# DeltaNet with a low-rank mixer on one core: the first two units multiply by Z inside the recurrence

## The chip, the core and the metric

The kernel runs on one core of a Trainium2 chip. The metric is the device time of one execution in microseconds. A measured time is the median of several runs. The profile is of one further execution. All numbers are FP32.

## The reference

For each of 4 batches and 8 heads, a delta rule runs over 768 tokens with a 48 x 48 state. Its output, with the heads side by side (384 columns), goes through a low-rank mixer over the tokens and a two-layer MLP over the channels.

```python
k_n = k / (norm(k) + 1e-6)
for t in range(S):
    y[t] = q[t] @ state
    v_old = k_n[t] @ state
    state = state + beta[t] * outer(k_n[t], v[t] - v_old)
x = heads_side_by_side(y)              # (4, 768, 384)
h = x.transpose(0, 2, 1) @ U @ V       # U: 768 x 32, V: 32 x 768
u = x + h.transpose(0, 2, 1)
out = u + maximum(u @ w_ch1, 0) @ w_ch2   # 384 -> 1536 -> 384
```

## The kernel before

**Chunks and units.** The 768 tokens of a batch are 12 chunks of 64. Six chunks are a unit, so units 0 and 1 are batch 0, units 2 and 3 are batch 1, and so on to unit 7. A unit's data live in one of two slots, which alternate. In each chunk the kernel forms k k^T (`pg`) and the masked k q^T (`qk`), inverts the triangular matrix that the delta rule gives (the result is called Z, 64 x 64 for each head and chunk; it overwrites `pg` and is then read as `zt`), and then runs over the chunks one after the other with the state.

**The inverse.** `blocks` solves 32 x 32 diagonal blocks, for units 0 to 2 as pairs of 16 x 16 blocks, by a chain of VectorE instructions (L803, L809) between two transposes (L794, L816). `joins` puts blocks together with small products. For units 0 and 1 two 16 x 16 blocks are joined by 64-row products in two diagonal quadrants of TensorE's array (L860 first, L874 second, 16 moving columns each). Two 32 x 32 blocks are then joined by L900, L903, L918 and L921. `part` and `diagonals` make copies on ScalarE for this. `place_of`, `begin` and `need` only say which step may follow which.

**Ahead of the recurrence.** `prepare`, called for each half of a unit (three chunks), multiplies by Z once: k^T Z (L1023, copied over `kq` by ScalarE) and Z v (L1034, copied over `vn` by ScalarE).

**The recurrence.** `recur` takes the 12 chunks of a batch in turn. For each chunk there is a product of the prepared keys with the old state (L1072), a subtraction from the prepared v on VectorE (L1085), which gives z, a product of k with z (L1100), and an addition to the state on VectorE (L1111). Beside it `outputs` makes the chunk's output: q with the old state (L983) and `qk` with z (L997), which accumulate in one bank, and two copies on ScalarE to X (L967).

**Heads and row halves.** Eight heads are named by j (2), par (2) and g (2). A product of 64 x 64 or 48 x 64 fills one quadrant of the 128 x 128 array: its input rows choose the row half, its output rows the column half. Before the change a head with par = 1 changes its row half on the way (`half(g ^ par)`), so that L1034 and L997 use all four quadrants. L1100 then needs k of those heads on the other half too, which is a second copy, `kz`, loaded by the loads named z.

**The MLP.** When batch 0's outputs are all in X, `front` applies the mixer (L1393, L1399, L1412) and transposes X for a group of 256 tokens (L1436, L1439). `channels` is the first layer (L1497), `narrow` the second, in fewer block products by sums of blocks (L1617). Batch 3 takes its own path (L1296). The weights come as 64-bit numbers and are converted to FP32 by ScalarE (L1198) and VectorE (L1212, L1219, L1226) in `load_weights`, in the first part of the execution.

**What sets the order.** Every piece of work is a generator, and a list written out in the file, `ORDER`, says at which of some 2250 places each generator takes its next step. The steps are issued in this order, so each engine's instructions, and each DMA queue's, stand in it. The times that the steps carry (`op("pe", 0.23, ...)`) were for a planner that made the list; in the build they decide nothing but the list's bookkeeping.

In the profile an FP32 product is two TensorE instructions and a transposition one, so a step of `recur` shows 16 matmuls, a block of L700 (`products`) 48, and one half's `prepare` 48 and 48.

## Time and profile before

| | |
|---|---|
| timed runs, median | 599.51 us (597.67 to 601.25, three runs) |
| the profiled execution | 596.6 us |
| its span in the profile | 594.9 us |
| mean granted TensorE clock | 0.943 |
| TensorE matmul busy | 559.7 us (94%), 10428 instructions |
| VectorE busy | 409.3 us (69%), 1011 instructions |
| ScalarE busy | 216.8 us (36%), 442 instructions |
| GpSimd busy | 133.3 us (22%), 229 instructions |
| DMA moved | 36.23 MB |

The page of the profile has 40 slices of the span, each with the busy tenths of every engine and the granted TensorE clock; groups of instructions by source line; and the chain of work that ended last, followed back from the end. Queries of the trace give the same for a window of time, and a timeline. PE is TensorE's matmuls and PEld its weight loads, DVE is VectorE, ACT ScalarE, POOL GpSimd, SP the queue that issues most DMAs. Matmuls are pipelined: a matmul's own duration is longer than the distance from its start to the next one's start.

### The profile page before, as it was taken

The page shows a single profiled execution, that of the slowest core. Times are in us where ns is not written, and L with a number is a line of the kernel's source. Part 1 is how long each engine was busy: PE and PEld are TensorE (multiplying, and loading weights), DVE is VectorE, ACT ScalarE, POOL GpSimd, SP SyncE. Part 2 cuts the span into 40 slices and gives each one's busy share as a digit, 9 for nine tenths or more (in the row PEclk, how much of TensorE's full clock was granted, in tenths as well). Part 3 has the DMA queues.
Part 4 walks back from the last instruction along what each step waited for, and adds up shares of the span by engine and source line. Part 5 has one row for each costly group of instructions (what it writes and reads, how often), then busy time and mean ns, then how long its engine had stood idle before and what let it go on. Part 6 is the DMA issues. An engine that isn't in the chain of part 4 may idle for free.

```text
span 594.9 us, 23426 instructions
## 1 busy us (share of the span) xinstructions
PE 559.7 (94%) x10428; PEld 481.6 (81%) x10428; DVE 409.3 (69%) x1011; ACT 216.8 (36%) x442; POOL 133.3 (22%) x229
## 2 busy tenths in 40 slices
PE   3778978899999999999999999999999999999997
PEld 3578977678988887989889887889899868656997
DVE  3888758899999458999884279998883235313542
ACT  1846475446322542035224341252243321335000
POOL 8122036116010724141205214520310000000000
PEclk9855556999999999999999999999999999999999
DMA  9981639714030415240402144420401000000000
GB/s 140 180 176 24 214 80 197 152 56 79 3 65 12 68 31 92 46 91 13 82 2 43 18 83 90 79 56 2 95 7 43 4 2 4 16 8 1 26 28 28
DMA packets 89445, 36.23 MB, mean 61 GB/s; under 512 B 75456, under 2 KB 87104, under 8 KB 89344
## 3 DMA queue, kind: packets, MB, share of 16 engines
q1 hardware_dynamic: 80800, 24.69, 20.7%
q0 software_dynamic: 6944, 9.74, 8.3%
q8 instruction: 82, 1.34, 1.0%
q10 hardware_dynamic: 1600, 0.30, 0.3%
q14 instruction: 19, 0.16, 0.1%
HBM read 29.98 MB, written 4.72 MB: 58 GB/s over the span
## 4 chain that ended last, share of the span: by engine, by line
PE 83%; DVE 11%; issue 2%; ACT 2%; DMA 1%; SPq 0%; DVEq 0%; ACTq 0%
PE P L1617 27%; PE P L1497 22%; PE P L1296 7%; PE P L700 4%; DVE xt L809 3%; DVE prod L803 3%; PE P L1072 2%; PE P L860 2%; PE P L874 2%; PE P L1023 2%; PE P L1034 2%; PE P L983 2%; PE P L997 2%; PE P L1100 2%; PE P L1412 2%
## 5 line engine op out<-in xcount | busy, mean ns | idle before, releaser
L1497 PE MATMUL P<-ut,w_sb 128*128 128x256 f32 x648 | 150.1, 385 | 1.5 <-ACT ut L1439 0.9
L1497 PEld LDWEIGHTS P<-ut,w_sb 128*128 128x128 f32 x648 | 119.9, 190 | 18.7 <-ACT ut L1439 1.1
L1617 PE MATMUL P<-w_sb,hs 128*128 128x192 f32 x540 | 96.7, 331 | 0.1
L1617 PEld LDWEIGHTS P<-w_sb,hs 128*128 128x128 f32 x540 | 87.2, 190 | 3.7 <-issue 1.2
L809 DVE TENSOR_TENSOR xt<-xt,prod 128x112 f32<-128x112 f32 (+21 forms) x200 | 64.6, 323 | 6.9
L803 DVE TENSOR_TENSOR prod<-gs,xt 128x112 f32<-128x112 f32 (+21 forms) x200 | 63.3, 316 | 3.5
L1537 DVE TENSOR_TENSOR X<-X,P 128x192 f32<-128x192 f32 x84 | 29.1, 349 | 49.8 <-PE P L1617 49.4
L1462 ACT ACTIVATE hs<-P 128x512 f32<-128x512 f32 x54 | 32.2, 598 | 77.5 <-PE P L1497 65.6
L967 ACT COPY X<-P 64x192 f32<-64x192 f32 x96 | 30.0, 313 | 66.3 <-PE P L997 63.4
L1617 PE MATMUL P<-w_sb,S 128*128 128x192 f32 x288 | 50.7, 330 | 0.0
L1617 PEld LDWEIGHTS P<-w_sb,S 128*128 128x128 f32 x288 | 46.6, 190 | 2.8 <-issue 1.8
L555 POOL DMA_DIRECT2D slot<-in_v_dram x32 | 21.1, 664 | 92.3 <-DVE prod L803 60.3
L1085 DVE TENSOR_TENSOR z<-slot,P 128x192 f32<-128x192 f32 x44 | 15.5, 352 | 30.8 <-PE P L1072 29.7
L541 POOL DMA_DIRECT2D slot<-in_q_dram x40 | 24.6, 621 | 46.9 <-DVE slot L747 33.3
L939 ACT COPY slot<-zz 32x384 f32<-32x384 f32 x64 | 32.4, 509 | 7.0 <-DVE zz L878 3.9
L700 PE MATMUL P<-slot 48*64 48x64 f32 x1536 | 30.9, 231 | 2.1 <-issue 1.4
L1296 PE MATMUL P<-slot,w_sb 128*128 128x384 f32 x96 | 32.9, 486 | 0.0
L700 PEld LDWEIGHTS P<-slot 48*64 48x64 f32 x1536 | 27.9, 144 | 5.6 <-issue 2.7
L946 POOL MEMSET slot<- 32x384 f32 x32 | 13.3, 421 | 84.2 <-PE P L903 63.4
L1617 PE MATMUL P<-w_sb,slot 128*128 128x192 f32 x180 | 30.4, 327 | 0.9 <-DVE X L1537 0.9
L555 POOL DMA_DIRECT2D slot<-in_k_dram x44 | 29.4, 670 | 8.3 <-PE P L1100 7.6
L1617 PEld LDWEIGHTS P<-w_sb,slot 128*128 128x128 f32 x180 | 29.3, 190 | 1.7 <-DVE X L1537 1.5
(153 smaller groups left out, 901.4 us busy)
## 6 DMA issues: line engine op xcount, KB each, us to landing
out_dram<-X SPq DMA_DIRECT2D x22, 192.0 KB, 2.7
w_sb<-in_moe_w_ch_dram SPq DMA_DIRECT2D x10, 384.0 KB, 5.6
slot<-in_k_dram SPq DMA_DIRECT2D x48, 72.0 KB, 3.9
slot<-in_k_dram POOLq DMA_DIRECT2D x44, 72.0 KB, 3.8
slot<-in_v_dram SPq DMA_DIRECT2D x32, 72.0 KB, 3.7
slot<-in_v_dram POOLq DMA_DIRECT2D x32, 72.0 KB, 3.5
X<-in_moe_w_ch_dram SPq DMA_DIRECT2D x6, 384.0 KB, 6.1
wide<-in_moe_w_ch_dram SPq DMA_DIRECT2D x6, 384.0 KB, 5.0
```

What stands on the lines that cost most here:

```text
L541: queue.dma_start(out=blocked(n)[quarter(y % 4), j, g, :, 0:w], in_=src[b, 4 * g + 2 * j + par, hf * UC * L : (hf + 1) * UC * L, BK * low ...
L555: queue.dma_start(out=t[half(1 - g if name == "z" else g), :, to, 0:D], in_=src[b, 4 * g + s, hf * UC * L : (hf + 1) * UC * L, :].rearrang ...
L700: nc.tensor.matmul(p_g[half(g ^ (par * i)), par, c], kq[rows, c, j, 0, half(g)], kq[rows, c, j, i, half(g)], start=True, stop=True,)
L803: nc.vector.tensor_tensor(out=prod, in0=gb[:, :, j : j + 1, j + 1 :].to_broadcast([128, split, m, w]), in1=xb[:, :, 0:m, j : j + 1].to_bro ...
L809: nc.vector.tensor_tensor(out=xb[:, :, 0:m, j + 1 :], in0=xb[:, :, 0:m, j + 1 :], in1=prod, op=ALU.subtract,)
L939: nc.scalar.copy(pg[quarter(i), :, at, :, a : a + BK], cut(zc, h)[quarter(i)].rearrange("p r (c j) t -> p r c j t", j=2),)
L967: nc.scalar.copy(x[half(c % 2), c // 2, 4 * D * g : 4 * D * (g + 1)].rearrange("p (j r d) -> p r j d", r=2, d=D), states(p_y)[half(g)],)
L1296: nc.tensor.matmul(to, w, t, start=start, stop=stop, skip_group_check=True)
L1462: nc.scalar.activation(hs[:, fs[0] : fs[1] + 1 : fs[1] - fs[0]], p_f, ACTF.Relu)
L1497: nc.tensor.matmul(p_f[:, x], w(x, t), ut[:, t], start=(t == 0), stop=(t == KT - 1))
L1537: nc.vector.tensor_tensor(out=to, in0=to, in1=p, op=ALU.add)
L1617: nc.tensor.matmul(to, of[0], of[1], start=of[2], stop=of[3], skip_group_check=True)
```

## The change

For units 0 and 1 (`DIRECT`) `prepare` does nothing. Instead `recur` multiplies by Z in each chunk, after the subtraction: z = Z (v - k S), one product of eight heads more, and a copy on ScalarE. For the same units (`NATURAL`) heads keep their row half from beginning to end; `kz` is not loaded, and the products of Z and of `qk` use two diagonal quadrants. The first join products of units 0 and 1 run on 32 moving columns instead of 16, of which the second 16 are read. The diagonal of `xt` is written by ScalarE in a step of its own, `spread`, for all units. The two masking instructions of a `qk` block become one. Two fillers are added: a product of the identity with itself, 256 columns, whose result is not read. The list `ORDER` is written anew for all steps (2253 instead of 2259): it begins with unit 0's k, and the recurrence of batch 0 begins straight after the joins of unit 0. The diff, without the list:

```diff
--- before.py
+++ after.py
@@ -141,210 +141,210 @@
+    FILLERS = (0, 1)
     ORDER = """
...
@@ -502,6 +502,8 @@
     TURNED = 3
     TURNED_K = 3
     SPLIT, QUARTERED = (0, 1), (2,)
+    DIRECT = (0,1)
+    NATURAL, ONCE = (0, 1), ()
     FIRST = dict(k1=11, q0=12, q1=13, z0=14, v0=15, z1=16, v1=17)
     FIRST = {(x[0], int(x[1])): y for x, y in FIRST.items()}
 
@@ -608,6 +610,13 @@
     def landed(name, n, j=1):
         return need(*[(name, n, g, j) for g in range(2)])
 
+    def spread(n):
+        yield op("act", 0.2)
+        nc.scalar.copy(
+            out=xt.rearrange("p s t -> p (s t)")[:, 0 : BK * BK : BK + 1], in_=cp[:, n % 2]
+        )
+        emitted(("spread", n), 0.06)
+
     def norms(n):
 
         _, _, _, _, _, vn, _, _ = units[n]
@@ -618,15 +627,13 @@
         norm = small.tile([128, BK], FP32, name="norm")
         nc.scalar.sqrt(norm, flat[:, 0 : BK * BK : BK + 1])
         yield need(("betas", hf))
-        yield op("dve", 1.25, port=True)
+        yield op("dve", 1.05, port=True)
         nc.vector.tensor_scalar_add(norm, norm, 1e-6)
         rec = small.tile([128, BK], FP32, name="rec", bufs=1)
         nc.vector.reciprocal(rec, norm)
         nc.vector.tensor_tensor(out=rec, in0=rec, in1=rec, op=ALU.mult)
         nc.vector.tensor_tensor(out=cp[:, n % 2], in0=rec, in1=betas[:, hf, b], op=ALU.mult)
-        nc.vector.tensor_copy(
-            out=xt.rearrange("p s t -> p (s t)")[:, 0 : BK * BK : BK + 1], in_=cp[:, n % 2]
-        )
+        begin(spread(n), 2)
         emitted(("c", n))
         yield op("dve", 0.2)
         rows = small.tile([128, BK], FP32, name="norm_rows")
@@ -698,7 +705,7 @@
                 for par, g in QUADS:
                     rows = half(par, D)
                     nc.tensor.matmul(
-                        p_g[half(g ^ (par * i)), par, c],
+                        p_g[half(g ^ (par * i * (n not in NATURAL))), par, c],
                         kq[rows, c, j, 0, half(g)],
                         kq[rows, c, j, i, half(g)],
                         start=True,
@@ -726,14 +733,13 @@
                         pg[:, :, :, j, at], even[:, y : y + 1],
                     )
             else:
-                for par in range(2):
-                    yield op("dve", dve(384), give=[("pair", x)] if par else ())
-                    nc.vector.tensor_tensor(
-                        out=qk[:, par, :, j],
-                        in0=p_g[:, par],
-                        in1=mask_u[:, None, :].to_broadcast([128, UC, L]),
-                        op=ALU.mult,
-                    )
+                yield op("dve", dve(768), give=[("pair", x)])
+                nc.vector.tensor_tensor(
+                    out=qk[:, :, :, j],
+                    in0=p_g,
+                    in1=mask_u[:, None, None, :].to_broadcast([128, 2, UC, L]),
+                    op=ALU.mult,
+                )
             emitted(("product", n, j, i), 0.1)
 
         def turn_blocks(j, i):
@@ -796,6 +802,7 @@
         yield need(("c", n), ("returned", n - 1))
         yield op("dve", dve(1024 // split), port=True)
         nc.vector.tensor_tensor(out=gb, in0=gb, in1=by, op=ALU.mult)
+        yield need(("spread", n))
         for j in range(size - 1):
             m, w = j + 1, size - 1 - j
             yield op("dve", 2 * dve(split * m * w) + 0.04, port=True)
@@ -848,25 +855,26 @@
                 else:
                     emitted(("parted", n, h))
                 words, mode = (48, "Q") if lone else (96, "J")
+                at = 0 if lone else SB
                 pb = lone and alone(n).rearrange("p c j t -> p (c j) t")
                 for y, e in enumerate(es):
                     if y % 6 == 0:
-                        got = yield op("pe", 0.69 if lone else 0.41, mode, take=None if y else "pair", words=words, flow=0.08 if lone else 0.16, cold=1.7 if lone else None)
+                        got = yield op("pe", 0.69 if lone else 0.41, mode, take=None if y else "pair", words=words, flow=0.16, cold=1.86 if lone else None)
                     if y == 0:
-                        x, p_e = got, one(got)[:, 0 : 12 * SB].rearrange("p (e t) -> p e t", e=12)
+                        x, p_e = got, one(got)[:, 0 : 12 * BK].rearrange("p (e t) -> p e t", e=12)
                     for rows in map(half, range(2)) if lone else map(quarter, range(4)):
                         a = rows.start % L
                         of = pb[rows, e] if lone else heads(pg)[rows, e, a : a + BK]
                         nc.tensor.matmul(
-                            p_e[rows, y], of, zc[rows, e, SB:BK], start=True, stop=True
+                            p_e[rows, y, at:BK], of, zc[rows, e, at:BK], start=True, stop=True
                         )
                 yield op("act", act(192), give=[("pair", x)], rush=True)
                 xe = xz[:, h].rearrange("p c (h t) -> p (c h) t", h=2)
-                nc.scalar.copy(xe, p_e)
+                nc.scalar.copy(xe, p_e[:, :, SB:BK])
                 yield need(("parted", n, h))
                 for y, e in enumerate(es):
                     if y % 6 == 0:
-                        got = yield op("pe", 0.69 if lone else 0.41, mode, take=None if y else "pair", words=words, flow=0.08 if lone else 0.16, cold=1.7 if lone else None)
+                        got = yield op("pe", 0.69 if lone else 0.41, mode, take=None if y else "pair", words=words, flow=0.08 if lone else 0.16, cold=1.86 if lone else None)
                     if y == 0:
                         x, p_d = got, one(got)[:, 0 : 12 * SB].rearrange("p (e t) -> p e t", e=12)
                     for rows in map(half, range(2)) if lone else map(quarter, range(4)):
@@ -990,10 +998,10 @@
                     )
                 emitted(("y1", b, c))
                 yield need(("z", b, c), ("b", b, c if cu == UC - 1 else c + 1))
-                yield op("pe", 0.23, "Q", words=32, flow=0.16)
+                yield op("pe", 0.35 if n in NATURAL else 0.23, "Q", words=32, flow=0.16)
             z = zs[c]
             for j, par, g in heads:
-                at = half(g ^ par)
+                at = half(g ^ par * (n not in NATURAL))
                 nc.tensor.matmul(
                     states(p_y)[half(g), par, j],
                     qk[at, par, cu, j],
@@ -1015,6 +1023,9 @@
 
             kn, kq, zt, _, _, vn, _, _ = units[n]
             yield need(("upper", n, h), ("diagonal", n, h), ("grams", n), ("scaled", n), *landed("k", n, 0), *landed("k", n))
+            if n in DIRECT:
+                emitted(("ready", n, h))
+                return
             cs = range(3 * h, 3 * h + 3)
             x = yield op("pe", 0.70, "Q", take="pair", words=96, flow=0.64)
             p_k = pair(x)[:, :, 0:384].rearrange("p g (c j t) -> p g c j t", c=3, j=2)
@@ -1032,7 +1043,7 @@
             for c in range(3):
                 for j, par, g in heads:
                     nc.tensor.matmul(
-                        p_v[half(g ^ par), par, c, j * D : j * D + D],
+                        p_v[half(g ^ par * (n not in NATURAL)), par, c, j * D : j * D + D],
                         zt[half(g), par, cs[c], j],
                         vn[half(g), cs[c], 2 * par + j],
                         start=True,
@@ -1057,20 +1068,21 @@
         yield need(("rec", NU * b - 1))
         for c in range(NC):
             n, cu = NU * b + c // UC, c % UC
-            kn, kq, _, _, _, vn, _, kz = units[n]
-            yield need(("ready", n, cu // 3), *landed("z", n))
+            kn, kq, zt, _, _, vn, _, kz = units[n]
+            direct = n in DIRECT
+            yield need(("ready", n, cu // 3), *landed("k" if n in NATURAL else "z", n))
             if cu == UC - 1:
                 begin(outputs(c, s_old), 2 if b == 0 else 60)
                 yield need(("y1", b, c))
             if c == 0:
                 zs[c] = vn[:, cu]
                 emitted(("b", b, c))
-            else:
+            if c > 0:
                 xb = yield op("pe", 0.23, "Q", take="pair", words=32, flow=0.16)
                 p_b = pair(xb)[:, :, 0 : 2 * D]
                 for j, par, g in heads:
                     nc.tensor.matmul(
-                        states(p_b)[half(g ^ par), par, j],
+                        states(p_b)[half(g ^ (0 if direct or n in NATURAL else par)), par, j],
                         kq[half(par, D), cu, j, 0, half(g)],
                         states(s_old)[half(par, D), g, j],
                         start=True,
@@ -1079,15 +1091,32 @@
                 emitted(("b", b, c))
                 if cu < UC - 1:
                     begin(outputs(c, s_old), 2 if b == 0 else 60)
-                yield need(("y", b, c - 3)) if c > 2 else []
+                yield need(("y", b, c - 3)) if c > 2 and not direct else []
                 yield op("dve", dve(192), give=[("pair", xb)])
-                z = zs[c] = small.tile([128, 4, D], FP32, name="z", bufs=3)
+                z = vn[:, cu]
+                if not direct:
+                    z = zs[c] = small.tile([128, 4, D], FP32, name="z", bufs=3)
                 nc.vector.tensor_tensor(
                     out=z.rearrange("p (r j) d -> p r (j d)", r=2),
                     in0=vn[:, cu].rearrange("p (r j) d -> p r (j d)", r=2),
                     in1=p_b,
                     op=ALU.subtract,
                 )
+            if direct:
+                xz = yield op("pe", 0.35 if n in NATURAL else 0.23, "Q", take="pair", words=32, flow=0.16)
+                p_z = pair(xz)[:, :, 0 : 2 * D]
+                for j, par, g in heads:
+                    nc.tensor.matmul(
+                        states(p_z)[half(g ^ par * (n not in NATURAL)), par, j],
+                        zt[half(g), par, cu, j],
+                        vn[half(g), cu, 2 * par + j],
+                        start=True,
+                        stop=True,
+                    )
+                yield need(("y", b, c - 3)) if c > 2 else []
+                yield op("act", act(192), give=[("pair", xz)], rush=True)
+                z = zs[c] = small.tile([128, 4, D], FP32, name="z", bufs=3)
+                nc.scalar.copy(z.rearrange("p (r j) d -> p r (j d)", r=2), p_z)
             emitted(("z", b, c))
             if c == 0:
                 begin(outputs(c, None), 2 if b == 0 else 60)
@@ -1096,10 +1125,10 @@
                 xs = yield op("pe", 0.23, "Q", take="pair", words=32, flow=0.16)
                 p_s = pair(xs)[:, :, 0 : 2 * D]
                 for j, par, g in heads:
-                    at = half(g ^ par)
+                    at = half(g ^ par * (n not in NATURAL))
                     nc.tensor.matmul(
                         states(p_s)[half(par, D), g, j],
-                        kz[at, cu, j] if par else kn[at, cu, 2 * j, 0:D],
+                        kz[at, cu, j] if par and n not in NATURAL else kn[at, cu, 2 * j + par, 0:D],
                         zs[c][at, 2 * par + j],
                         start=True,
                         stop=True,
@@ -1439,6 +1468,13 @@
         nc.scalar.copy(to, p_u)
         emitted(("front", b, i), 0.1)
 
+    def filler(k):
+        x = yield op("pe", 0.44, "F", take="pair", words=4, flow=0.427)
+        nc.tensor.matmul(
+            one(x)[:, 0:256], ident, ident[:, None, :].to_broadcast([128, 2, 128]), start=True, stop=True
+        )
+        free["pair"][x] = state["now"] + 0.06
+
     def reserve():
 
         yield [("x", 0, NC - 2)]
@@ -1648,11 +1684,13 @@
             begin(grams(n, 1), place_of(n) + 3)
             begin(blocks(n), place_of(n))
             for y, name in enumerate("bkqvz" if n >= TURNED_K else "kqvz"):
-                if n or y:
+                if (n or y) and not (name == "z" and n in NATURAL):
                     for some in ((0,), (1,)) if n < NU else ((0, 1),):
                         begin(load(n, name, some), FIRST.get((name, n), 20 + 4 * n + y))
         begin(load_weights(), 40)
         begin(reserve(), 0)
+        for k in FILLERS:
+            begin(filler(k), 0)
         begin(weight_sums(), 97)
         begin(token_sums(), 3)
         begin(first_of_last(), 94)
```

405 lines of the change are left out of this document (202 added, 203 removed).

## The prediction

> **What bounds the kernel now.** I read the page's 40 slices first, then the busy time by stretch, the groups of single lines, the timeline of a few microseconds, and the chain that ended last. The slices show an ending that is full and a beginning that is not:
>
> ```profile
> PE   3778978899999999999999999999999999999997
> PEclk9855556999999999999999999999999999999999
> ```
>
> A slice is 14.9 us. From slice 8 on TensorE is busy at full clock; in slices 3 to 6 it is nearly as busy, but the granted clock is half. The same by stretch (length, then busy time and instructions of PE, weight load, DVE, ACT, POOL, then the clock):
>
> ```profile
> core 0: us, PE busy (x) PEld busy (x) DVE busy (x) ACT busy (x) POOL busy (x), PEclk, DMA share, GB/s
> 0.00:34.20 34.20, 17.12 (x386) 14.94 (x386) 21.48 (x73) 15.94 (x30) 15.69 (x33) 0.92 1.13 169
> 34.20:50.50 16.30, 14.82 (x433) 14.45 (x433) 13.35 (x38) 10.20 (x22) 6.00 (x11) 0.50 0.51 100
> 50.50:58.30 7.80, 7.09 (x246) 6.81 (x243) 7.22 (x21) 4.11 (x6) 1.74 (x3) 0.50 0.18 42
> 58.30:86.40 28.10, 25.52 (x804) 24.40 (x808) 19.44 (x36) 16.33 (x36) 2.60 (x6) 0.50 0.46 144
> 86.40:107.80 21.40, 16.93 (x613) 14.69 (x605) 16.45 (x31) 13.24 (x25) 12.13 (x20) 0.76 0.87 197
> 116.00:500.00 384.00, 380.40 (x7393) 330.16 (x7394) 290.40 (x723) 133.63 (x274) 92.53 (x155) 1.00 0.23 46
> ```
>
> From 116 us PE idles 3.6 us in 384. The built order of both kernels has the same 494 PE steps from `channels b0 i0 e0` on, with the same 138 changes between full-array and quadrant work, so I give that part no gain and no loss. What the change can move is the start of the first L1497 product, now at 115.95 us, and everything behind it shifts by as much.
>
> Before it lie: start-up to 34.2 (loads, then DVE's substitution of unit 0), the joins of unit 0, `prepare` of unit 0, the joins of unit 1 mixed with the recurrence of batch 0, the rest of the recurrence, the front. The chain shows what carries these:
>
> ```profile
> 3.89 4.96 DMA slot<-in_k_dram
> 18.66 1.98 DVE gs L794
> 34.19 5.30 PE P L860 x96
> 55.76 1.28 PE P L1023 x45
> 57.04 1.25 PE P L1034 x45
> ```
>
> L860, a 64x64 product in one of two diagonal quadrants with 16 moving columns, takes 5.30 us for 96, so 55 ns each. L1023 and L1034, the same size in all four quadrants, take 1.28/45 = 28 ns. Both are at half clock. So a quadrant accepts one instruction each 107 to 110 ns whatever moves through it, and two quadrants give half the rate of four. Full clock shows the same ratio: L588 in two quadrants takes 0.70 us of starts for 24 (29 ns), L1072 in four 14 ns. This is my price for all products that the change puts on two quadrants.
>
> One recurrence step at half clock:
>
> ```profile
> 97.26 0.68 PE L983 MATMUL P<-s,slot 48*64 48x48 f32 x16
> 97.35 0.35 DVE L1085 TENSOR_TENSOR z<-slot,P 128x192 f32<-128x192 f32 x1 [0.40 <-PE P L1072]
> 97.75 0.58 PE L1100 MATMUL P<-z,slot 64*48 64x48 f32 x16
> 98.49 0.35 DVE L1111 TENSOR_TENSOR s<-s,P 128x192 f32<-128x192 f32 x1
> 98.98 0.68 PE L1072 MATMUL P<-s,slot 48*64 48x48 f32 x16 [0.22 <-DVE s L1111]
> ```
>
> L1072 starts at 96.53 and again at 98.98: 2.45 us for state product, DVE, update product, DVE. L983 and L997 fill PE's waits.
>
> **The change part by part** (against the profiled execution: span 594.9, 596.6 us in all).
>
> *Start-up.* The new order issues unit 0's k first: its second SP load is the second in that queue, not the fifth (issue at 1.6 instead of 3.89 us; the landing then took 4.96 us). PE's first transposes can start near 6 us, not 9.05, but unit 1's k and the second pair of heads still have to land (fifth to seventh on SP, 3.9 to 5.3 us plus about 5). L794 needs only unit 0's two products; I put it at 16 to 17 us, not 18.66. Two L713 (0.4 us each) and L603 (0.3) of other steps then stand in front of the norms on DVE, while weight conversions (1.0 us in all) leave the substitution. Joins of unit 0 start 2.2 us earlier (bounds 0 and 4): **-2.2**. The two fillers are full-array products on 256 columns: like L1497 (223 ns a start at full clock), two instructions each, 0.9 us at half clock. The first lies in the wait for unit 1's k; the second in a stretch in which PE idled 2.73 us before L860. Zero; uncovered, 0.9 us each.
>
> *First join products on 32 columns.* L700 moves 64 columns at the same 28 ns in four quadrants as L983 moves 48, and L860 moves 16 at the two-quadrant rate, so the quadrant's 107 ns hides 32: zero.
>
> *Unit 0 to unit 1's joins.* Before, 24.1 us from 34.2 to 58.26. `prepare` of unit 0 goes: 192 instructions at 27 ns, 5.1 us. In its place chunk 0 gets its Z product and its output in two quadrants (0.85 each) and its update (0.43) ahead of unit 1's joins: net -3.0. Three L700 blocks now lie in this stage instead of two (1.3): -1.7. And unit 1's joins wait for L816 of unit 1 (2.0 us), which waits for unit 0's last join copies. I take **-1.5** (bounds -3.0 and 0).
>
> *Joins of unit 1 and chunks 1 to 5.* PE was busy 25.5 of 28.1 us here. Added: five Z products, 16 instructions at 53 ns, 4.3 us; five outputs from 0.43 to 0.85, 2.1 us; gone: one L1023 block, 1.3 us. Net 5.1, of which I let idle time swallow 1.5: **+3.6** (bounds 2.0 and 5.1).
>
> *Chunks 6 to 11.* Here the chain decides. Z comes behind the DVE subtraction: 0.85 of starts and 0.25 of drain (0.68 less 0.43 in L983), then an ACT copy like L865 (0.32) and two handovers of 0.05: 1.52 us a chunk, so 2.45 becomes 3.97. Six times: 9.1. The copy also queues on ACT behind weight conversions (L1198, 0.92), as L967 does. Gone is unit 1's `prepare`, which stretched three chunks from 2.45 to 3.7, 2.9 and 3.1: 2.4 us. Once the transposes of unit 2 have run the clock is 1.0, as at 103.5 before: -1.0. Net **+5.7** (bounds 2 and 8).
>
> *The rest.* The front's tt copy (L1399) now stands behind three substitution steps of unit 2 on DVE, where before there was none: 1.3 us, of which I let 1.0 lie beside the front's first products L1393 (2.1): **+0.3**. The eight z loads, ACT's prepare copies (0.8 and 0.64), the diagonal copy moved from DVE to ACT (0.2 each, which DVE awaits only after the 0.65 of L798) and the two mask products made one are off the chain: zero. If ACT is late, each of eight copies costs at most 0.2.
>
> Sum: -2.2 - 1.5 + 3.6 + 5.7 + 0.3 = +5.9, so 602.5 for an execution like the profiled one. That one lies 2.9 below the median of the timed runs (599.51; 597.67 to 601.25). Part of this is luck that I already withhold from the new kernel: the clock stood at 1.0 from 86.4 to 93.2 amid the recurrence. I add 1.0 for the rest: **603.5 us**.
>
> **The clock.** It changes on a grid of 3.41 us. The stretch from 83.0 held L1023 x48 and 72 other small products and was followed by 1.0; the stretches from 52.3 and 55.7, with 20 and 15% less streamed through the array, were followed by 0.5. The profile's stretch from 60 to 70 us has PE busy 10.00 us of 10 at 0.50. The Trainium skill, "TensorE: Matmul & The Clock Gate", part 1, says that one window of about 3.4 us of sustained busy work gives the full clock. The trace disagrees, if busy is read as the busy row: ten busy microseconds of small products got none. I go by the amount streamed.
>
> **The rivals.**
>
> A, *the clock rises and stays* (faster). In the new order two blocks of L700 and all 32x32 joins of unit 0 stand close together just before chunk 0; they stream about as much per 3.41 us as the stretch at 83.0. If the clock rises there and 32-column joins keep it, the 31 us of joins and chunks 1 to 5 shrink to about 21, bound by the chain: -10, so 593.5. It decides if three or more grid stretches between 45 and 80 us show 1.0. Against it: a chunk with five products streams 5/4 of before's, but in 3.97 instead of 2.45 us, and before's was too little. Chance 0.15. By the skill's rule above this would be the likely case.
>
> B, *two quadrants run as fast as four* (near no change). Then Z and outputs cost 0.43 instead of 0.85: 2.1 + 2.1 us less in chunks 1 to 5, 6 x 0.43 = 2.6 less on the chain, 0.8 at chunk 0: 596. L860 and L588 against L983 speak against it. The Trainium skill, same page, part 3 ("What overlaps and what doesn't"), says that a weight load overlaps running products only when its row group differs. By that rule four quadrants, with two row groups, gain nothing over two diagonal ones, which is this rival; the 55 against 27 ns disagree. Chance 0.10.
>
> C, *the earlier start pays for it*: start-up at -4, `prepare` at -3.0, joins at +2.0, chain at +5: 0.3 over the profiled execution with the front's term, with the 1.0 some 598 to 601. Chance 0.17.
>
> D, *ACT becomes the bound of the chain*: a conversion of 0.92 and two output copies of 0.31 before each Z copy would make a chunk 5 us: +6 more, 609. ACT was busy 13.2 of 21.4 us there, so some of this is likely, all of it not. Chance 0.08.
>
> My forecast keeps 0.50.
>
> **How the numbers follow.** A measurement of this kernel can tell about 0.5% (3 us) from no change. Faster than 596.5: nearly all of A and a third of B, 0.18. Within 596.5 to 602.5: C, the rest of B, and the lowest fifth of the forecast, 0.35. Slower: 0.47. The range 595 to 609 leaves out most of A and the tail of D.
>
> **What would show it.** L1497's first start near 121 us (119 to 125). New Z products of 16 in 0.85 us of starts at half clock; if 0.43, B. Update to update near 4 us in chunks 6 to 9, not 2.45. The clock at 0.50 from about 35 to 105 us; if 1.0 for ten of them, A. First join products 55 ns with 32 columns. PE from the first L1497 to the end unchanged within 2 us: if that part moves by more, the place of my whole sum is wrong.

## The result, and the profile after

The changed kernel takes 603.14 us (median of 22 runs, 599.47 to 605.02), the kernel before 599.89 us (22 runs, 595.18 to 602.75): a ratio of 1.0059, 95% interval 1.0038 to 1.0079. It is slower by about 3 us, where 603.5 was forecast. The profiled execution after took 603.8 us with a span of 601.8; before, 596.6 and 594.9.

The slices of the page after, TensorE and its granted clock:

```profile
PE   5888898999999999999999999999999999999997
...
PEclk9655555899999999999999999999999999999999
```

A slice is now 15.0 us. The stretch at half clock is one digit longer than before and TensorE is busier in it. The same by stretch, cut where start-up, unit 0's joins, unit 1's joins with chunks 1 to 5, chunks 6 to 11 and the front end (columns as before the change):

```profile
core 0: us, PE busy (x) PEld busy (x) DVE busy (x) ACT busy (x) POOL busy (x), PEclk, DMA share, GB/s
0.00:32.60 32.60, 20.57 (x342) 17.59 (x343) 20.99 (x70) 13.34 (x26) 16.36 (x34) 0.82 0.82 129
32.60:55.20 22.60, 20.56 (x578) 19.80 (x580) 20.12 (x55) 14.49 (x31) 4.36 (x8) 0.50 0.39 106
55.20:86.00 30.80, 28.71 (x758) 27.26 (x752) 20.04 (x36) 16.13 (x37) 1.65 (x4) 0.50 0.51 159
86.00:113.90 27.90, 23.69 (x605) 21.32 (x606) 19.87 (x33) 14.92 (x34) 6.49 (x10) 0.62 0.50 108
113.90:123.20 9.30, 7.96 (x147) 5.52 (x147) 7.03 (x23) 3.57 (x8) 6.56 (x11) 0.85 0.65 115
123.20:500.00 376.80, 373.77 (x7348) 325.15 (x7349) 286.37 (x701) 132.81 (x276) 94.81 (x159) 1.00 0.25 48
```

The first product of the first layer (L1497 before, L1533 now) starts at 123.19 us, 7.24 later than at 115.95. Behind it nothing has changed: 478.9 us before, 478.6 after.

| us, from the two traces | before | after | difference | forecast |
|---|---|---|---|---|
| start to unit 0's first join | 34.20 | 32.55 | -1.65 | -2.2 |
| to unit 1's first join | 24.06 | 22.61 | -1.45 | -1.5 |
| to the update of chunk 5 | 27.3 | 31.0 | +3.6 | +3.6 |
| to the last output product | 22.0 | 27.5 | +5.5 | +5.7 |
| to the first L1533 | 8.35 | 9.59 | +1.2 | +0.3 |

The sum is +7.2 between these two executions, of which the one before lies 3.3 us below its median and the one after 0.7 above its own. The medians differ by 3.25.

A chunk of the second half, from the timeline after (start, duration, engine, line; in brackets the idle time and what ended it):

```profile
92.47 0.74 DVE L1241 TENSOR_SCALAR w_sb<-power 128x768 int32<-128x768 int32 x1
...
92.61 1.09 PE L1109 MATMUL P<-slot 64*64 64x48 f32 x16
...
93.25 0.96 DVE L1248 SCALAR_TENSOR_TENSOR w_sb<-w_sb 128x768 int32<-128x768 int32 x1
93.77 0.32 ACT L1119 COPY z<-P 128x192 f32<-128x192 f32 x1 [2.62 <-PE P L1109]
...
94.14 0.57 PE L1129 MATMUL P<-z,slot 64*48 64x48 f32 x16 [0.45 <-ACT z L1119]
...
94.50 0.95 PE L1005 MATMUL P<-z,slot 64*64 64x48 f32 x14
94.78 0.35 DVE L1140 TENSOR_TENSOR s<-s,P 128x192 f32<-128x192 f32 x1 [0.58 <-PE P L1129]
```

The Z product (L1109) and ScalarE's copy stand in the chain as forecast, 1.53 us from 92.61 to 94.14. Updates follow each other in 3.9 to 4.1 us up to chunk 9; the last takes 7.6, because unit 2's transposes and products stand before it, as they did before the change (7.0). Note the two conversions of weights on DVE (L1241, L1248): they run while Z is formed.

### The profile page after: what moved, and what is told of

It is laid out like the page before. It is cut to its first block, busy times and chain, and to the rows that moved or that the text cites. A ratio compares the mean times of both kernels' runs of the same rounds, so it can differ in the third digit from the quotient of the medians.

```text
span 601.8 us, 23034 instructions
## 1 busy us (share of the span) xinstructions
PE 572.9 (95%) x10240; PEld 494.1 (82%) x10240; DVE 409.8 (68%) x987; ACT 216.2 (36%) x454; POOL 130.2 (22%) x225
## 4 chain that ended last, share of the span: by engine, by line
PE 87%; DVE 8%; issue 2%; ACT 1%; DMA 1%; SPq 0%; DVEq 0%; ACTq 0%
PE P L1653 28%; PE P L1533 22%; PE P L1325 7%; PE P L707 4%; PE P L1005 3%; PE P L1084 3%; PE P L1129 2%; DVE xt L816 2%; PE P L991 2%; DVE prod L810 2%; PE P L868 2%; PE P L882 2%; PE P L1109 2%; PE P L1034 1%; PE P L1465 1%
## 5 line engine op out<-in xcount | busy, mean ns | idle before, releaser
L1533 PE MATMUL P<-ut,w_sb 128*128 128x256 f32 x648 | 150.5, 385 | 1.0 <-ACT ut L1468 0.9
L1533 PEld LDWEIGHTS P<-ut,w_sb 128*128 128x128 f32 x648 | 119.8, 190 | 18.5 <-ACT ut L1468 1.1
L816 DVE TENSOR_TENSOR xt<-xt,prod 128x112 f32<-128x112 f32 (+21 forms) x200 | 64.6, 323 | 6.9
L1498 ACT ACTIVATE hs<-P 128x512 f32<-128x512 f32 x54 | 32.1, 598 | 71.2 <-PE P L1533 59.2
L1140 DVE TENSOR_TENSOR s<-s,P 128x192 f32<-128x192 f32 x40 | 14.0, 351 | 29.0 <-PE P L1129 27.2
L1099 DVE TENSOR_TENSOR z<-slot,P 128x192 f32<-128x192 f32 x33 | 11.5, 349 | 31.9 <-PE P L1084 31.7
```

Source lines behind the costliest of these rows:

```text
L816: nc.vector.tensor_tensor(out=xb[:, :, 0:m, j + 1 :], in0=xb[:, :, 0:m, j + 1 :], in1=prod, op=ALU.subtract,)
L1498: nc.scalar.activation(hs[:, fs[0] : fs[1] + 1 : fs[1] - fs[0]], p_f, ACTF.Relu)
L1533: nc.tensor.matmul(p_f[:, x], w(x, t), ut[:, t], start=(t == 0), stop=(t == KT - 1))
```

## The experiments

The stages are those of the table above, read from one trace of each kernel: the first join of unit 0 and of unit 1, the update of chunk 5, the last output product, the first product of the first layer, and what is left from there to the end.

| | joins 0 | joins 1 | chunk 5 | last output | first layer | left |
|---|---|---|---|---|---|---|
| before | 34.20 | 58.26 | 85.6 | 107.60 | 115.95 | 478.9 |
| after | 32.55 | 55.16 | 86.1 | 113.60 | 123.19 | 478.6 |
| four_quadrants | 32.41 | 54.67 | 84.3 | 109.09 | 117.76 | 478.9 |
| no_z | 30.44 | 52.58 | 79.6 | 105.24 | 114.56 | 481.6 |
| before_row_half | 32.60 | 56.46 | 84.2 | 106.22 | 114.34 | 479.7 |
| before_z_inside | 32.79 | 56.66 | 88.6 | 115.99 | 124.10 | 485.3 |
| no_fillers | 33.77 | 56.25 | 87.3 | 114.89 | 123.12 | 480.1 |
| fq_prepare | 32.75 | 56.68 | 85.9 | 113.24 | 122.78 | 481.3 |
| after_prepare | 32.70 | 57.88 | 87.5 | 115.11 | 124.44 | 481.6 |
| fq_direct0 | 31.67 | 53.83 | 83.7 | 109.54 | 127.04 | 485.8 |
| direct0 | 32.51 | 55.21 | 84.8 | 114.37 | 131.65 | 485.8 |

**four_quadrants: the changed kernel with heads changing their row half again.**

```diff
-    NATURAL, ONCE = (0, 1), ()
+    NATURAL, ONCE = (), ()
...
+    for at, name in ((211, "load n1 namez halves(0,)"), (153, "load n1 namez halves(1,)"), (119, "load n0 namez halves(1,)"), (112, "load n0 namez halves(0,)")):
+        ORDER[at:at] = [name] * 2
```

> The changed kernel with one part undone: heads with par = 1 change their row half again, so Z products and outputs of units 0 and 1 use four quadrants, and the second copy of k is loaded again (eight loads). Two quadrants are the price (the forecast's row, 55 against 27 ns): each Z product and each output falls from 0.85 to 0.43 us of starts at half clock; 2.1 + 2.1 us in chunks 1 to 5, 6 x 0.43 = 2.6 on the chain, 0.8 at chunk 0, so 5 to 8 us less than the changed kernel, 595 to 598. If two quadrants run as fast as four (rival B), or if the new order is what costs, it stays within 2 us of the changed kernel, 601 to 605.

599.35 us, ratio to before 1.0008 (0.9981 to 1.0036): 3.8 us less than the changed kernel, where 5 to 8 were expected. The whole loss of the change is gone, though Z is still inside the recurrence. Groups of matmuls between 55 and 108 us of this kernel, the Z product and the output (in the fence after it, the same two of the changed kernel between 55 and 112 us):

```profile
L1113 PE MATMUL P<-slot 64*64 64x48 f32 x164 | 7.3, 299 | 1.2 <-DVE slot L1103 0.5
...
L1009 PE MATMUL P<-z,slot 64*64 64x48 f32 x144 | 6.0, 304 | 1.3 <-issue 1.3
```

```profile
L1109 PE MATMUL P<-slot 64*64 64x48 f32 x164 | 10.8, 294 | 1.0 <-DVE slot L1099 0.5
L1005 PE MATMUL P<-z,slot 64*64 64x48 f32 x146 | 9.9, 303 | 1.3 <-issue 1.3
```

One product lasts as long (299 and 294 ns, 304 and 303), yet the busy time of the group falls from 10.8 to 7.3 and from 9.9 to 6.0 us, since more of them run at once. Of these 7.4 us the path gave back 4.5 by the last output (113.60 to 109.09), and the medians 3.8. Chunks 6 to 11 gave back the 2.6 us that were priced (27.5 to 24.8); unit 1's joins with chunks 1 to 5 gave back only 1.4 of 4.2 (31.0 to 29.6), though TensorE's busy time there fell by 3.1 us (28.71 to 25.64). A pause of 1.2 us named "issue", which the changed kernel's trace doesn't have there, takes most of what is missing from those 3.1.

**no_z: the changed kernel with the Z product and its copy in the recurrence left out** (so the state is not the reference's).

```diff
-                    nc.tensor.matmul(
-                        states(p_z)[half(g ^ par * (n not in NATURAL)), par, j],
-                        zt[half(g), par, cu, j],
...
-                z = zs[c] = small.tile([128, 4, D], FP32, name="z", bufs=3)
-                nc.scalar.copy(z.rearrange("p (r j) d -> p r (j d)", r=2), p_z)
+                z = zs[c] = vn[:, cu]
```

> The changed kernel without the multiplication by Z in the recurrence of units 0 and 1: neither the product nor ScalarE's copy is issued, z is v - kS itself. This leaves a part of the computation out. If the chain is what the change lengthened, a chunk goes from about 4.0 to 2.45 us: 9.1 us over chunks 6 to 11, 4.3 of PE time in chunks 1 to 5, 1 at chunk 0; 12 to 15 us less than the changed kernel, 588 to 591. If the earlier start and the order decide and the chain is covered (rival C), 3 to 8 us less, 595 to 600.

599.15 us, ratio 1.0003 (0.9977 to 1.0029). Far from the 588 to 591 that the price list gave, and inside the 595 to 600 that were named for a covered chain (rival C). Up to chunk 5 the price held: from unit 1's first join, 27.0 us instead of 31.0, and five Z products were priced at 4.3. From there to the last output it did not: 25.7 us instead of 27.5, where 9.1 were priced. The timeline of this kernel, one chunk:

```profile
85.94 1.01 DVE L1232 TENSOR_SCALAR w_sb<-power 128x768 int32<-128x768 int32 x1
...
86.07 0.57 PE L1120 MATMUL P<-slot 64*48 64x48 f32 x16
...
86.98 0.96 DVE L1239 SCALAR_TENSOR_TENSOR w_sb<-w_sb 128x768 int32<-128x768 int32 x1
87.86 0.35 DVE L1131 TENSOR_TENSOR s<-s,P 128x192 f32<-128x192 f32 x1
...
88.26 0.68 PE L1084 MATMUL P<-s,slot 48*64 48x48 f32 x16 [0.77 <-DVE s L1131]
```

The update product L1120 is done at 86.64; the addition to the state, which needs only that, starts at 87.86, because the two conversions of weights stand before it in DVE's order. In the changed kernel the same two lines (L1241, L1248) lay under the Z product and its copy. So Z's 1.5 us on the chain was in good part time in which DVE did work that must be done in this stretch anyway. What was gained was partly lost once more behind the first layer's start, where the work is the same (481.6 us instead of 478.6). The waits of TensorE between 134 and 145 us, where the changed kernel's TensorE idled 0.1 us from 133 to 150:

```profile
PE P L929 <- issue: 2.0, 1, 2.0
PE P L1045 <- issue: 1.9, 1, 1.9
```

**before_row_half and before_z_inside: one part of the change alone, in the order of before.** The first leaves heads on their row half and drops the z loads of units 0 and 1; the second puts Z into the recurrence of units 0 and 1, on four quadrants, and empties `prepare` but for chunk 0's Z v.

```diff
+    NATURAL = (0, 1)
-                at = half(g ^ par)
+                at = half(g ^ par * (n not in NATURAL))
...
+    ORDER = dict(enumerate(x for _, x in sorted(ORDER.items()) if not x.startswith(("load n0 namez", "load n1 namez"))))
```

```diff
+    DIRECT = (0, 1)
-            for c in range(3):
+            for c in range(3) if n not in DIRECT else ():
...
+                if n in DIRECT:
+                    for j, par, g in heads:
+                        nc.tensor.matmul(
+                            states(p_b)[half(g ^ par), par, j],
+                            zt[half(g), par, cu, j],
+                            vn[half(g), cu, 2 * par + j],
...
+                    nc.scalar.copy(z.rearrange("p (r j) d -> p r (j d)", r=2), p_b)
```

> The kernel before, in its own order, with one part of the change: heads stay on their row half in units 0 and 1, no second copy of k; Z is still multiplied ahead. Two quadrants as price: 12 outputs cost 0.43 us more each and the four Z v products in prepare 1.28 more each at half clock, 5.1 + 5.1 us on PE, of which half lies in waits: 3 to 7 us more than before, 603 to 607. If two quadrants cost nothing, or the eight loads less pay for it, within 2 us of before, 598 to 602.

> The kernel before, in its own order, with the other part: units 0 and 1 multiply by Z inside the recurrence, right behind the subtraction, on four quadrants; prepare issues nothing for them but chunk 0's Z v. Gone: 10.2 us of prepare's products at half clock, of which 5.1 stood ahead of unit 1's joins and 3.7 in chunks 1 to 8. Added: a chunk's chain gets 0.43 + 0.25 + 0.32 + 0.1 = 1.1 us, 6.6 us over chunks 6 to 11, and 2.1 us of PE time in chunks 1 to 5. By the forecast's sum these cancel: 598 to 602. If the chain is covered, 5 us less than before; if Z in the recurrence is the whole loss of the changed kernel, 4 us more.

before_row_half: 597.89 us, ratio 1.0001 (0.9966 to 1.0036), so nothing, where 603 to 607 were expected. Its outputs do cost TensorE more, as the groups between 56 and 103 us show (below it the same group of the kernel before, between 58 and 105 us):

```profile
L999 PE MATMUL P<-z,slot 64*64 64x48 f32 x144 | 8.5, 284 | 0.0
```

```profile
L997 PE MATMUL P<-z,slot 64*64 64x48 f32 x144 | 6.0, 295 | 0.0
```

In that order the extra 2.5 us do not show in the time. Whether they lie beside waits is not shown: the granted clock was also 1.0 for 17.0 us between 50 and 100 us here, and for 6.9 in the trace before.

before_z_inside: 613.13 us, ratio 1.024 (1.0194 to 1.0286), 11 us above the range that the sum gave and 9 above the worst case named. The chain that ended last of this kernel (start, length, what carried it), around the place where `prepare` of unit 0 had stood:

```profile
32.78 5.30 PE P L861 x96
...
54.63 1.99 DVE zz L817
56.66 2.63 PE P L861 x45
```

Unit 1's joins start 23.87 us after unit 0's, against 24.06 with `prepare`: the 5.1 us of products that went gained 0.2. DVE's transpose L817 ends the wait there, not TensorE. In the recurrence TensorE stands still for 2.3 us in all before the Z products, which this kernel issues in one step with the subtraction, so that no other product can stand between the two. The last output comes 8.4 us later than before. Another 6.4 are lost behind the first layer's start, where the work is the same: behind 125 us TensorE's gaps of over 0.05 us make 8.4 us against 4.4 before (the longest 2.28, named "issue"), and right behind that longest gap the clock fell to half for 3.4 us, at 155.3. Nothing in the trace ties the gaps to Z.

**Fillers against the cold clock.** Three kernels add 90 to 105 products of the identity with itself (the traces have 180 instructions of them in before_warm and 210 in the two others; the 71 of the expectation is too low), 128 columns on the full array, between the small products of units 0 and 1: after_warm to the changed kernel, before_warm to the one before, fq_warm to four_quadrants. They write columns 384 to 512 of a bank that the kernel uses too, so some of its sums change.

```diff
+            if s["e"] == "pe":
+                for _ in range(fillers(y, i, s)):
+                    nc.tensor.matmul(P[:, 0, 384:512], ident, ident, start=True, stop=True, skip_group_check=True)
```

> The changed kernel with 71 more fillers that nothing reads (identity times identity, full array, 128 columns, 0.21 us at full clock, 0.43 at half): eight before the first join product of unit 0, one behind each early PE step, two behind each first or second join step and one behind each 32x32 step of units 0 and 1, one behind each state, Z and update product of batch 0. Theory: the half clock from 31 to 106 us is the price of Z there, and it follows the amount streamed through the array. Then the clock stays at 1.0 through most of this, chunks 1 to 5 with unit 1's joins shrink from 31 to about 21 us, chunks 6 to 11 from 28 to about 21, unit 0's joins by 3: 583 to 590. Rival: VectorE, ScalarE and the weights' conversions bind there, PE's clock does not: the fillers change little or cost up to 5 us, 601 to 608.

> The kernel before with the same fillers at the same places (it has no Z product in the recurrence, so 12 fewer). Theory: its joins and recurrence at half clock gain as well, but less, since its chain is shorter: 10 to 15 us less than before, 585 to 590, and the distance between the two kernels at full clock is under 2 us. Rival as for the changed kernel: 599 to 605.

> The changed kernel with four quadrants and the second copy of k, with the same fillers. Theory: at full clock two quadrants cost 0.46 instead of 0.23 us a product, half of what they cost at half clock: 2 to 3 us less than the changed kernel with fillers, 581 to 587. Rival: the same time as the changed kernel with four quadrants alone, 598 to 604.

658.48, 634.26 and 652.69 us: ratios 1.1017 (1.0982 to 1.1051), 1.0518 (1.0454 to 1.0583) and 1.0895 (1.0856 to 1.0933). Neither the theory nor the rival was right: the added products cost 36 to 55 us against the kernels without them. Busy time of after_warm from 60 to 80 us, and what its engines waited for between 60 and 100 us:

```profile
60.00:80.00 20.00, 20.00 (x346) 16.81 (x346) 11.18 (x19) 7.15 (x14) 1.79 (x4) 0.50 0.16 46
```

```profile
ACT z L1133 <- PE P L410: 11.4, 2, 7.1
...
DVE s L1154 <- PE P L410: 7.3, 1, 7.3
```

TensorE is busy 20.00 us of 20 and the clock is still 0.50. The clock was 1.0 from 26.9 to 50.8 us, then half until 160. In these 20 us 26 instructions of the fillers (L410), two for each, take 9.6 us, and the chain's copies and additions wait for them. So after_warm and fq_warm (half clock from 56.1 to 155.1 us) don't say what the half clock costs. In before_warm's profiled execution (625.5 us, the fastest of four) the clock was 1.0 from 69.5 to 110.5 us. From unit 1's joins to the update of chunk 5 it still took 31.5 us, against 27.3 at half clock without the added products, which take 14.5 of those 31.5.

**no_fillers: the changed kernel without its two fillers, first join products on 16 columns again.**

```diff
-        nc.tensor.matmul(one(x)[:, 0:256], ident, ident[:, None, :].to_broadcast([128, 2, 128]), start=True, stop=True)
...
-at = 0 if lone else SB
+at = SB
```

> The changed kernel without its two fillers and with 16 columns in the first join products of units 0 and 1. The forecast priced both at nothing: within 1.5 us of the changed kernel, 601 to 605. If their purpose, a higher clock in one or two stretches, is reached in the changed kernel, 2 to 4 us more, 605 to 607.

604.17 us, ratio 1.0099 (1.0073 to 1.0125), against 1.0059 (1.0038 to 1.0079) with them: a hint of 2 us in their favour, but the intervals meet. From unit 0's joins to the update of chunk 5 it takes 53.5 us, with them 53.6: 32 columns cost nothing and gain nothing.

**Z ahead in the new order.** fq_prepare has `prepare` for both units and four quadrants; after_prepare the same on two; fq_direct0 and direct0 keep Z inside for unit 0 alone. The steps of `prepare` were put into the new order by hand, those of Z taken out; a step whose banks are not free yet waits for the next place. The diff is that of fq_prepare; the two with direct0 have `DIRECT = (0,)`, after_prepare and direct0 keep `NATURAL` at (0, 1).

```diff
-    DIRECT = (0,1)
+    DIRECT = ()
-    NATURAL, ONCE = (0, 1), ()
+    NATURAL, ONCE = (), ()
...
+    for y, names in (
...
+        (402, ('prepare n1 h1', 2)),
+        (398, ('prepare n1 h1', 2)),
...
+        (355, ('prepare n1 h0', 4)),
+        (346, None),
...
+        ORDER[y : y + (names is None)] = [names[0]] * names[1] if names else []
```

> The new order, fillers and 32 columns, but Z ahead of the recurrence and four quadrants for both units, as before (the second copy of k is loaded again). Theory 1 (the new order alone is worth about what it looked like against Z inside in the old order): clearly faster than before, 590 to 595 us. Theory 2 (Z inside and the new order belong together; the order gains by having no block of prepare ahead of unit 1's joins): 597 to 601, with unit 1's joins starting at 57 us or later.

> The new order, four quadrants; Z inside the recurrence for unit 0 only, unit 1 prepared ahead. The price list says: chunks 6 to 11 lose six Z terms of 1.5 less 0.4 us each (four quadrants), -6.6, and get unit 1's prepare, four blocks of 1.3 = 5.1 us, of which half lies in the chain's own gaps: -4, so 594 to 596. If other waits take Z's place on the chain, as they did where Z was left out altogether, 598 to 601.

> The changed kernel with Z inside for unit 0 only; unit 1 is prepared ahead, on two quadrants for Z v (2.7 us for 48) and four for the keys. Price list: six Z terms of 1.5 us gone, 9.1, and 8 us of prepare, half of it in gaps: -5, so 598 us. If other waits take Z's place: 602 to 605.

> The changed kernel with Z ahead for both units, two quadrants for Z v and for the outputs. Against the one with Z inside for unit 0 only, unit 0's stretch swaps five Z products (4.3 us, two quadrants) for 8 us of prepare, while TensorE has no idle time there: +3.5, so 601 to 603 by the price list. If TensorE is not what sets the end there, the same as with Z inside for unit 0 only.

605.14 us (1.0134, 1.0103 to 1.0165), 615.35 (1.0319, 1.0280 to 1.0358), 617.91 (1.0366, 1.0329 to 1.0403) and 607.61 (1.0168, 1.0132 to 1.0204): all slower than their twins with Z inside, and above everything expected. The two with Z inside for unit 0 alone can't be read to the end: a bank pair that the front wants came free later in my order. The first layer's first product waits 8.83 us for DVE's masking L770, which frees it, and the chain of direct0 passes through unit 2's substitution on DVE before the first layer starts at 131.65 us:

```profile
117.14 0.70 DVE gs L837
120.93 0.95 DVE X L1479
128.10 1.95 DVE zz L856
```

Up to the last output they can be read: 109.54 and 114.37 us, against 109.09 and 113.60 with Z inside for both units. Six Z terms off the chain gained nothing there either. The two with `prepare` for both lose in the stage where the forecast put the gain: from unit 0's to unit 1's joins they take 23.93 and 25.18 us, against 22.26 and 22.61. Both also pause 2.1 us near 145 us, and some 2.4 to 3 us of their loss lie behind the first layer's start.

## Why the prediction was right

The forecast named the right time, the right direction, and for four of five stages a term within 0.6 us. That the time came out to 0.4 us is in part luck: between the two traces the sum is +7.2 us, where +5.9 was forecast, and between the medians it is +3.25. The allowance of 1.0 had to stand for the 3.3 by which the profiled execution before lay below its median. The rivals fell by their own marks. A: the clock was 0.5 from 31.3 to 106.4 us without a break. B: in chunks 1 to 9 the 16 starts of L1109 stretch over 0.75 to 0.91 us, in four_quadrants over 0.38 to 0.56, and four_quadrants is faster by 3.8 us. C: the start gained 1.65 and `prepare` 1.45, not 4 and 3. D: ScalarE was busy 14.92 of 27.90 us, and TensorE waited only 1.7 us in all for its Z copy.

The runs confirm less of the reasons than of the sum.

*Start-up.* -2.2 forecast, -1.65 between the two traces. But before_z_inside has the loads of before and starts its joins at 32.79, and no_z has the loads of after and starts at 30.44. Of kernels with the order of before the three traces have 34.20, 32.60 and 32.79, mean 33.2; with the order and fillers of after the seven have 30.44 to 32.75, mean 32.1. The step's own mark was met: the transpose L794 (L800 now) started at 16.96 us, where 16 to 17 was named and 18.66 was before. By the means the new start is worth about 1 us, but they are of one execution a kernel, which spread by 1.6 and 2.3 us.

*Unit 0's to unit 1's joins.* -1.5 forecast, -1.45 measured, and the caution in the step was its best part: the prediction held back gain because unit 1's joins wait for L816. In the old order taking `prepare` away gives 0.2 of 5.1 us. In the new one it gives 1.7 on four quadrants (23.93 to 22.26) and 2.6 on two. The reason is on DVE: counted from unit 0's first join, that transpose of unit 1 ends after 23.9 us before and 23.8 in before_z_inside, but after 22.1 in the changed kernel and 22.2 in fq_prepare. In the old order unit 1's joins could start no sooner, with or without `prepare`. The new order has this transpose 1.8 us earlier, and only then do the products of `prepare` stand in the way.

*Unit 1's joins and chunks 1 to 5.* +3.6 and +3.6. TensorE is busy 28.71 of 30.80 us here. Without Z the stage takes 4.0 us less, five Z products having been priced at 4.3. The other price did not hold as well: with four quadrants it takes 29.6 instead of 31.0, 1.4 us less, where five Z products and five outputs at half their cost were priced at 4.2.

*Chunks 6 to 11.* +5.7 and +5.5, but this step was right by its sum alone. It said that Z's 1.52 us a chunk adds 9.1. Leaving Z out gives 1.8. The step that failed is the claim that the chain 2.45 us long would otherwise stand free: even with no Z the new order's chunks take 25.7 us here, 3.7 more than before's 22.0. Two things that differ are weight conversions on DVE, which stand before the state's additions, and the clock, which had been 1.0 from 86.4 to 93.2 before. On the chain that ended last, within this stage, Z's product and copy carry 5.9 us of the changed kernel and DVE's conversions 2.2. Without Z the conversions carry 4.0, with four quadrants 6.0, and before the change 1.0. Two quadrants are worth 2.6 of the 5.5 (24.8 us with four). How the other 2.8 divide between Z, the order and the clock isn't settled.

*The clock.* The prediction named before's 6.9 us of full clock luck in part. The traces of the kernels without added products show that it goes with `prepare`. Between 35 and 99 us the clock was 1.0 for 3.4 to 17.0 us in all six that have blocks of `prepare` for unit 0 or 1 (before, before_row_half, fq_prepare, after_prepare, fq_direct0, direct0), and never in the five without (after, four_quadrants, no_z, before_z_inside, no_fillers). So the change took the full clock out of this part together with `prepare`. What that alone is worth no run separates.

*The rest.* +0.3 and +1.2, with the wrong mechanism. The prediction had the tt copy queue behind three substitution steps on DVE. The timeline after shows it waiting for TensorE:

```profile
113.83 2.82 PE L679 MATMUL P<-ident,slot 128*128 128x128 f32 x12
116.58 2.14 PE L1422 MATMUL P<-X,u_sb 128*32 128x384 f32 x24
```

```profile
118.79 0.56 DVE L1428 COPY tt<-P 128x384 f32<-128x384 f32 x1 [1.46 <-PE P L1422]
```

The same place before the change:

```profile
107.75 0.87 PE L672 MATMUL P<-ident,slot 128*128 128x128 f32 x6
108.55 2.14 PE L1393 MATMUL P<-X,u_sb 128*32 128x384 f32 x24
110.62 0.87 PE L672 MATMUL P<-ident,slot 128*128 128x128 f32 x6
```

```profile
111.28 0.55 DVE L1399 COPY tt<-P 128x384 f32<-128x384 f32 x1
```

All twelve transposes of this step of unit 2 (L679) now stand before the mixer's first product; before, six did (0.87 us at full clock), and six stood behind it, under DVE's work. The clock fell to half for 3.4 us just there, at 113.2. Counted from the last output, L1422 starts 2.0 us later than L1393 did, of which the steps behind it gave back 0.8.

Where, then, does the loss of 0.6% come from? The grid of runs answers for the two parts, and their signs depend on the order:

| ratio to before | Z ahead, four | Z ahead, two | Z inside, four | Z inside, two |
|---|---|---|---|---|
| order of before | 1 | 1.0001 | 1.024 | not run |
| new order | 1.0134 | 1.0168 | 1.0008 | 1.0059 |

In the new order Z inside is a gain of 1.1 to 1.3%, in the old one a loss of 2.4%, about half of it ahead of the first layer. The new order costs 1.3% if Z stays ahead. The two together come out even, and what is left, 0.5%, is the two quadrants: TensorE is busy 7.4 us longer there, in exchange for eight loads, whose own price no run measures. Since the steps of my mixed orders were placed by hand, and before_z_inside has its Z products where TensorE must wait for them, the sizes in the first two columns of the new order's row and the 2.4% of the old order are those of one placement each. No run was clearly faster than the kernel before.

## What to carry to other kernels

A term added to a dependency chain costs its length only if the other engines have nothing queued that must run in that time; look at what stands before the chain's next instruction on each engine, since it moves into the open when the term goes. A change of work and an order made for it can't be priced apart: run each part in both orders. Where a stage is full on one engine, leaving a piece of work out gave back nearly its price (4.0 of 4.3 us), but halving the cost of the same products gave back a third (1.4 of 4.2). Give such terms bounds too, and chain terms the widest.

## What the runs showed of the hardware that was not expected

*The clock follows how much of the array works.* I summed, for each stretch of 3.41 us of the clock's grid in every trace, the moving columns of the matmuls times the share of the 128 x 128 array that each fills. The first layer's full-array products, 256 columns every 223 ns, make some 3,900. Of 63 stretches at half clock that were followed by full clock, 55 held 1,400 or more and the other eight 944 to 1,332. Of 286 that were followed by half clock, 284 held less than 1,365 and the other two 1,404 and 1,536. So it is a tendency and no sharp limit. By this count the stretches from 52.3 and 55.7 us, which the prediction put 20 and 15% below the one from 83.0 (1,572), lie 30 and 20% below it. Rival A's argument counted 32x32 joins as if each filled a quadrant: the stretch of the changed kernel at 48.3 us makes some 1,700 that way but 1,066 by array share, and stayed at half. Between 35 and 98 us no stretch of the five kernels without `prepare` makes more than 1,140. The Trainium skill, "TensorE: Matmul & The Clock Gate", part 1, lets one window of sustained busy work raise the clock; 20.00 busy us of 20 at 0.50 in after_warm disagree, if busy is read as the profile's busy time.

*Small pauses differ from trace to trace.* Pauses of TensorE that the profile names "issue" make 4.7 us in the trace before, 2.7 after, 7.6 in no_z, 7.1 in fq_prepare, 6.4 in before_z_inside; single ones last up to 2.3 us, and those behind 125 us lie in work that is the same in all. What causes them, and whether they belong to a kernel or to one execution, no run here shows, since each kernel has one trace. They are as large as the effect that was to be measured.

*The start is not sharp.* Up to unit 0's joins, no_z and the changed kernel issue the same work in the same order, and reach them at 30.44 and 32.55 us.
